# Linear attention and gated FFN on one core: a new step order from block 1 on, q's halves combined by reductions, six weight chunks reloaded

## The chip, the core and the metric

One core of a Trainium2 chip runs the whole program. Its engines work beside each other, each on its own list of instructions, in order: TensorE (PE in the profile, with PEld for its weight loads), VectorE (DVE), ScalarE (ACT), GpSimd (POOL) and SyncE (SP). Semaphores order them against each other. In this kernel SP issues loads from the inputs, writes of split weights to DRAM and writes of the output; POOL issues the loads that bring split weights back from DRAM. The metric is the device time of one launch in microseconds; 1039.9 is the median of three runs of the kernel before.

## The reference

`reference.py`, cut to what is computed (batch 8, 8 heads, 576 rows, head size 64; 4608 tokens, d_model 512, d_ff 1536; all fp32):

```python
q_s = softmax(q, axis=-1)          # over the head size
k_s = softmax(k, axis=2)           # over the 576 rows
kv = einsum('bhsd,bhde', k_s, v)   # 64 x 64 per head
x = einsum('bhsd,bhde->bhse', q_s, kv)       # laid out as 4608 x 512
xn = x / sqrt(mean(x * x) + 1e-6) * rms_g
out = (silu(xn @ w_gate) * (xn @ w_val)) @ w_out
```

Both softmaxes subtract the maximum and divide by the sum plus 1e-9.

## The kernel before

**Tiles.** The 4608 tokens are nine blocks of 512. d_ff is cut in 12 chunks of 128; a chunk holds its columns of w_gate and w_val and its rows of w_out. Operands of large matmuls are split into a high part (the value rounded to fp32r, by a copy: steps named `_hi`) and a low part (the rest, by a subtraction: steps named `_lo`), and a product is three matmuls: high x high, high x low, low x high.

**The order.** No scheduler decides at build time. A string, `ORDER`, names some 3,100 steps one after the other, and a loop calls the function of each; `tc.manual_schedule()` keeps that order on every engine. A step reads `name.numbers`, and `:A`, `:D` or `:P` at its end puts it on ACT, DVE or POOL. So the string decides both where a piece of work runs and what stands ahead of it in its engine's list. If an instruction waits, all that stands behind it on its engine waits too.

**Stages.** Blocks 0 to 2 go one by one. For block j and chunk i the number is s = 12 j + i: `f1.s.0` and `f1.s.1` (L954) are the gate and value products, 12 matmuls each; `g_mul`, `silu`, `h_mul`, `h_hi`, `h_lo` make the hidden tile h; `f2.s` (L991) adds 12 matmuls with w_out into four PSUM banks of the output. `store.j.t` (L997) then scales tile t of the four into an SBUF tile `ot`, which has **two** buffers, and SP writes it out. In block 0 the weights are also unpacked. `w_hi`, `w_lo`, `o_hi`, `o_lo` split a chunk into the tiles `w` and `o` (two buffers each), in every one of the three blocks anew. During block 1 `w_keep` and `o_keep` write the split chunks to DRAM (`wd`, `od`), and `s_add`, `s_hi`, `s_lo`, `s_keep` prepare sums of weight quarters in DRAM for what follows.

Blocks 3 to 8 go as three pairs p = 0, 1, 2, with seven products in place of eight (Strassen-Winograd). `t_add`, `b_hi`, `b_lo` build the operands from x (after `x_nm`, the product of x with the norm's row); `pp.p.i.m.k` (L1095) is product k of chunk pair i, for gate (m = 0) or value (m = 1), six matmuls. `c_s1`, `c_u2` and the other `c_` steps add products (L1116), which frees their PSUM banks. `gate`, `hm`, `hp_hi`, `hp_lo` make h, `f2p.p.t.c` (L1182) is the output product of block t of the pair with chunk c, and `put.p.t.n` copies output tile n into `ot`, with the same two buffers. `w_in` and `o_in` (L1068, L1080) bring the split weights from DRAM, issued by POOL.

**Attention beside it.** While PE is on one block, the attention of later blocks runs in between. k: `k_max` (DVE), `k_tr` (a transpose on PE), `k_top` (DVE), `k_diag` (ACT or DVE), `k_rows` (PE, L549), `k_sub`, `k_exp`, then `k_mm` (PE) makes kv. q comes in with each head's 64 numbers on two groups of 32 partitions, so its maximum and sum are found for each half (`q_max`, `q_sum`), the other half's are fetched from the neighbouring partitions by four small reductions (`q_half`, `q_half2`, L707) and the two are combined: `q_max2` (L715) by a tensor_tensor, `q_sum2` (L733) by a scalar_tensor_tensor that also adds 1e-9. `q_sub`, `q_exp`, `q_rec`, `q_mul`, `q_t`, `q_hi`, `q_lo` follow, `q_x` (PE) makes x, and `x_sq`, `x_acc`, `n_hi`, `n_lo`, `n_sum` and the `n_` steps the norm.

Of the kernel before, what the change touches and what calls it, by code (L numbers as in the profile page):

```python
# [90 lines left out]
k_eps.2.0 h_mul.12 store.0.2:A s_add.1.1:P store.0.3:D h_hi.12:A k_rec.2.0 s_hi.0.4:A q_lo.2.0:P w_hi.14.0.2:A
s_keep.0.3 f1.13.1 g_mul.13 h_lo.12:P kv_hi.2.0:A k_load.2.2 silu.13 kv_lo.2.0 s_hi.1.1:A s_lo.0.4:P o_hi.13:A f2.12
h_mul.13 w_hi.15.0.2:A w_lo.14.0:P s_keep.0.4 h_hi.13:A k_diag.2.1:A w_lo.14.1:D v_ones.2.2 v_load.2.2 s_lo.1.1:P
k_rows.2.1 o_hi.14:A f1.14.0 k_sub.2.1 o_lo.13:P k_exp.2.1 s_keep.1.1 h_lo.13:D o_keep.13 w_lo.15.0:P q_x.2.0 k_max.2.2
w_keep.14 k_mm.2.1 w_lo.15.1:P x_hi.2.0:A g_mul.14 x_sq.2.0 f1.14.1 k_load.2.3 x_lo.2.0 silu.14 s_add.1.2:P k_eps.2.1
k_rec.2.1 w_keep.15 o_lo.14:P s_hi.1.2:D kv_hi.2.1:A k_tr.2.2 f2.13 h_mul.14 s_lo.1.2:P o_keep.14 kv_lo.2.1 h_hi.14:A
k_top.2.2 s_add.1.3:P k_diag.2.2:A s_keep.1.2 h_lo.14:D v_ones.2.3 k_rows.2.2 s_hi.1.3:A f1.15.0 v_load.2.3 k_sub.2.2
s_add.1.4:P o_hi.15:A k_exp.2.2 s_lo.1.3:P w_hi.16.0.2:D f1.15.1 k_max.2.3 w_lo.16.0:P s_keep.1.3 s_hi.1.4:A g_mul.15
w_lo.16.1:P silu.15 q_sub.2.1:P k_tr.2.3 w_keep.16 k_mm.2.2 k_top.2.3 s_lo.1.4:P f2.14 k_eps.2.2 k_load.3.0 q_exp.2.1
h_mul.15 k_rec.2.2 o_lo.15:P h_hi.15:D s_keep.1.4 w_hi.17.0.2:A q_sum.2.1 h_lo.15:P o_keep.15 f1.16.0 o_hi.16:A  # L100
q_half2.2.1 k_diag.2.3:A w_lo.17.0:P kv_hi.2.2:A q_sum2.2.1 q_rec.2.1 kv_lo.2.2 w_lo.17.1:P k_rows.2.3 g_mul.16 f1.16.1
q_mul.2.1:P k_sub.2.3 w_keep.17 silu.16 s_add.2.1:D v_ones.3.0 v_load.3.0 q_t.2.1 o_lo.16:P s_hi.2.1:A f2.15 h_mul.16
q_hi.2.1:A s_lo.2.1:P w_hi.18.0.2:A k_max.3.0 q_load.3.0 h_hi.16:A q_lo.2.1:P k_exp.2.3 k_tr.3.0 f1.17.0 k_top.3.0
h_lo.16:P o_hi.17:A s_add.2.2:D k_diag.3.0:A w_lo.18.0:P s_keep.2.1 s_hi.2.2:D q_x.2.1 g_mul.17 o_keep.16 s_lo.2.2:P
k_rows.3.0 silu.17 x_hi.2.1:D f1.17.1 k_sub.3.0 w_lo.18.1:P s_keep.2.2 x_sq.2.1 s_add.2.3:D w_keep.18 k_exp.3.0
# [221 lines left out]
def linear_attention_then_gated_ffn(ctx: ExitStack, tc, q, k, v, w_gate, w_val, w_out, rms_g, out):  # L327
# [375 lines left out]

    def other_half(st):
        sw = small.tile([P, M], F32, name="sw")
        for a in range(4):
            nc.vector.tensor_reduce(out=sw[32 * (a ^ 1):32 * (a ^ 1) + 32], in_=st[32 * a:32 * a + 32].unsqueeze(2),  # L707
                                    axis=AX.X, op=ALU.max)
# [522 lines left out]
```

## Time and profile before

| what | us |
|---|---|
| median of three runs | 1039.9 |
| lowest and highest | 1037.01 and 1043.96 |
| the profiled execution | 1044.21 |
| its span, first to last instruction | 1042.5 |

The mean granted TensorE clock in the profiled execution was 0.967 of full speed. The page of the profile lists each engine's busy time and cuts the span into 40 equal slices, each a digit for tenths. The view by windows gives busy time, count of instructions and granted clock in stretches that one chooses. Timelines give start, length, engine, line, operation and tiles; the bracket behind a row tells how long the engine was idle before it and whose signal ended the wait. A group of instructions reads: busy us, mean ns of one, then idle time before them. PE's busy time is of pipelined matmuls whose ends are modelled; how fast it goes is better read from starts, as with the row of twelve matmuls that the prediction shows.

### The profile page before, as it was taken

To read this page: it belongs to the slowest core of one execution; us is meant where nothing else is said; L and a number is where in the kernel's file an instruction comes from. 1 tells how busy PE (TensorE), PEld (TensorE's weight loads), DVE (VectorE), ACT (ScalarE), POOL (GpSimd) and SP (SyncE) were. 2 spreads that over 40 slices of the span, in tenths; PEclk is the share of its full clock that TensorE was granted. 3 is DMA by queue.
4 is the path that set the end of the run, shared out by engine and by line. 5 is a ranking of instruction groups with operands and counts; after the bars stand their busy time and mean duration, and the time that the engine had idled before them with its cause. 6 is when DMAs were issued, how large, how long until landed. Compare 5 with 4: busy or idle time off the path is not lost.

```text
span 1042.5 us, 14185 instructions
## 1 busy us (share of the span) xinstructions
PE 971.2 (93%) x4681; PEld 773.5 (74%) x4681; DVE 739.7 (71%) x1460; ACT 467.3 (45%) x705; POOL 574.8 (55%) x575
## 2 busy tenths in 40 slices
PE   8999998999799898879999999979999899999997
...
PEclk8999997999899999889999999989999999999999
...
GB/s 240 246 295 159 104 87 206 330 274 236 236 163 114 132 57 108 110 174 215 205 201 192 214 231 171 166 149 196 182 190 174 232 182 223 201 186 202 117 162 141
DMA packets 164100, 192.88 MB, mean 185 GB/s; under 512 B 105620, under 2 KB 127164, under 8 KB 159420
## 3 DMA queue, kind: packets, MB, share of 16 engines
...
q8 instruction: 37, 0.61, 0.2%
...
## 4 chain that ended last, share of the span: by engine, by line
PE 56%; DVE 20%; DMA 10%; issue 5%; POOL 3%; ACT 3%; SPq 3%; DVEq 0%; POOLq 0%; ACTq 0%
PE ps_gv L1095 13%; PE ps_o L1095 10%; PE ps_gv L954 8%; PE ps_o L1182 8%; PE ps_a L1095 5%; PE ps_o L991 3%; PE ps_a L1182 3%; DMA out_dram<-ot 3%; PE ps_gv L1182 3%; DMA vt<-in_v_dram 2%; DVE hh L389 2%; DMA qt<-in_q_dram 2%; DVE tmp L1116 1%; SPq L635 1%; DVE sw L707 1%
## 5 line engine op out<-in xcount | busy, mean ns | idle before, releaser
L954 PE MATMUL ps_gv<-xh,w 128*128 128x512 f32 x576 | 198.7, 412 | 3.7 <-DVE gs L959 2.0
L1095 PE MATMUL ps_gv<-x,ring 128*128 128x512 f32 x576 | 150.1, 406 | 14.8 <-DVE tmp L1116 8.8
L1095 PEld LDWEIGHTS ps_gv<-x,ring 128*128 128x128 f32 x576 | 110.4, 195 | 40.5 <-DVE tmp L1116 10.3
L954 PEld LDWEIGHTS ps_gv<-xh,w 128*128 128x128 f32 x576 | 112.6, 196 | 31.4 <-DVE gs L966 2.3
L954 PE MATMUL ps_gv<-xl,w 128*128 128x512 f32 x288 | 116.6, 408 | 0.0
L1116 DVE TENSOR_TENSOR tmp<-tmp,ps_gv 128x512 f32<-128x512 f32 x84 | 57.3, 683 | 48.5 <-PE ps_gv L1095 47.0
L1068 POOL DMA_DIRECT2D ring<-wd x54 | 30.0, 556 | 109.4 <-PE ps_o L1095 42.9
L877 POOL TENSOR_TENSOR w<-w,w 128x512 fp32r<-128x512 f32 x61 | 82.4, 1360 | 10.2 <-ACT w L389 5.0
L1095 PE MATMUL ps_o<-x,ring 128*128 128x512 f32 x360 | 86.8, 394 | 0.0
L389 ACT CAST hh<-gs 128x512 fp32r<-128x512 f32 x38 | 23.5, 619 | 126.3 <-DVE gs L1152 104.4
L1095 PEld LDWEIGHTS ps_o<-x,ring 128*128 128x128 f32 x360 | 68.6, 191 | 14.6
L991 PE MATMUL ps_o<-o,hh 128*128 128x512 f32 x256 | 66.5, 401 | 3.1 <-ACT hh L389 2.6
L954 PEld LDWEIGHTS ps_gv<-xl,w 128*128 128x128 f32 x288 | 57.0, 198 | 11.7 <-issue 0.6
L991 PEld LDWEIGHTS ps_o<-o,hh 128*128 128x128 f32 x256 | 47.2, 189 | 14.4 <-ACT hh L389 3.0
L1080 POOL DMA_DIRECT2D o<-od x36 | 20.5, 571 | 66.4 <-PE ps_o L1182 37.6
L1116 DVE TENSOR_TENSOR tmp<-tmp,ps_o 128x512 f32<-128x512 f32 x42 | 28.7, 685 | 30.0 <-PE ps_o L1095 29.4
L1068 POOL DMA_DIRECT2D w<-wd x18 | 10.0, 555 | 60.6 <-PE ps_a L1095 35.8
L975 POOL TENSOR_TENSOR hl<-gs,hh 128x512 fp32r<-128x512 f32 x24 | 32.3, 1344 | 18.4 <-ACT hh L389 16.8
L885 POOL TENSOR_TENSOR o<-w,o 128x512 fp32r<-128x512 f32 x30 | 40.3, 1344 | 1.3 <-ACT o L389 0.8
L1182 PE MATMUL ps_o<-o,hh 128*128 128x512 f32 x144 | 38.2, 398 | 2.6 <-DVE hh L389 2.6
L520 DVE TENSOR_REDUCE cm<-kt 116x128 f32<-116x640 f32 x28 | 36.7, 1309 | 3.4 <-DMA kt<-in_k_dram 3.3
L755 POOL TENSOR_TENSOR ql<-qT,qh 128x512 fp32r<-128x512 f32 x24 | 32.2, 1345 | 11.2 <-ACT qh L389 7.2
...
## 6 DMA issues: line engine op xcount, KB each, us to landing
...
ring<-wd POOLq DMA_DIRECT2D x18, 1024.0 KB, 5.3
w<-wd POOLq DMA_DIRECT2D x18, 1024.0 KB, 5.3
...
```

Of the source, the lines that this page charges most:

```text
L389: (e.copy if e is nc.scalar else e.tensor_copy)(dst, src)
L520: nc.vector.tensor_reduce(out=cm, in_=kt_[b, g].rearrange("p h j d -> p h d j"), axis=AX.X, op=ALU.max)
L755: on(nc.gpsimd).tensor_tensor(out=ql, in0=qT_[j, g], in1=qh_[j, g][0].bitcast(F32), op=ALU.subtract)
L877: on(nc.gpsimd).tensor_tensor(out=w[:, :, 1], in0=halves(s % NF, a, 1)[:, 0], in1=w[:, :, 0].bitcast(F32), op=ALU.subtract)
L885: on(nc.vector).tensor_tensor(out=ol, in0=W(s % NF, 2), in1=oh.bitcast(F32), op=ALU.subtract)
L954: nc.tensor.matmul(pd[s], lhsT=w[:, a, c // 2, m, c % 2 * P:c % 2 * P + P], rhs=X[j, c][x], start=(n == 1), stop=(n == 3 * NKT))
L975: on(nc.gpsimd).tensor_tensor(out=hl, in0=g_[s], in1=h_[s][0].bitcast(F32), op=ALU.subtract)
L991: nc.tensor.matmul(po[t], lhsT=a[:, t * P:(t + 1) * P], rhs=w, start=(i == 0 and n == 0), stop=(i == NF - 1 and n == len(terms) - 1))
L1068: nc.gpsimd.dma_start(t, src.rearrange("p a b f -> p (a b f)"))
L1095: nc.tensor.matmul(abc[b], lhsT=src[:, h, c * P:(c + 1) * P], rhs=operand(o, c, x), start=first and n == 0, stop=n == 5, skip_group_check= ...
L1116: nc.vector.tensor_tensor(out=dst, in0=ux[u + (src,)], in1=abc[b], op=ALU.add)
L1182: nc.tensor.matmul(pa[p, t, k], lhsT=a[:, k * P:(k + 1) * P], rhs=w, start=(c == 0 and n == 0), stop=(c == NF - 1 and n == 2))
```

## The change

The constants, tile sizes, pools and all matmuls stay. Three things change.

1. `ORDER` is another list from block 1 on (the steps before `h_mul.11` are the same): other places for most steps, and other engines for some 330 of them.
2. `q_max2` and `q_sum2` become reductions: the own and the other half's numbers stand beside each other in one tile, and for the sum a third column holds 1e-9 in three tiles that are kept.
3. The steps `w_hi`, `w_lo`, `o_hi` and `o_lo` of chunks 30 to 35 (the last six of block 2) are left out of the list. In their place `w_back` and `o_back` load the split chunks that block 1 wrote to DRAM. Both functions stood in the file, unused.

```diff
-k_tr.2.0 s_add.0.1:D h_hi.11:A q_hi.2.0:A w_lo.12.1:D s_hi.0.1:A s_add.0.2:D f1.12.0 w_keep.12 s_lo.0.1:D s_hi.0.2:A
+k_tr.2.0 h_hi.11:A w_lo.12.1:D f1.12.0 w_lo.13.1:D w_keep.12 k_top.2.0 s_add.0.1:D k_diag.2.0:A w_lo.13.0:D s_hi.0.1:A
...
-hp_lo.2.1.11:D f2p.2.1.11 put.2.1.0:D put.2.1.1:A put.2.1.2:D put.2.1.3:A
+put.2.0.2:D hp_lo.2.1.11:D f2p.2.1.11 put.2.0.3:A put.2.1.0:D put.2.1.1:D put.2.1.2:D put.2.1.3:A
...
     def q_max(j, g):
-        st = small.tile([P, M], F32, name="st")
-        nc.vector.tensor_reduce(out=st, in_=qt_[j, g], axis=AX.X, op=ALU.max)
+        st = small.tile([P, M, 2], F32, name="st")
+        nc.vector.tensor_reduce(out=st[:, :, 0], in_=qt_[j, g], axis=AX.X, op=ALU.max)
         st_[j, g] = st
 
     def other_half(st):
-        sw = small.tile([P, M], F32, name="sw")
         for a in range(4):
-            nc.vector.tensor_reduce(out=sw[32 * (a ^ 1):32 * (a ^ 1) + 32], in_=st[32 * a:32 * a + 32].unsqueeze(2),
+            nc.vector.tensor_reduce(out=st[32 * (a ^ 1):32 * (a ^ 1) + 32, :, 1], in_=st[32 * a:32 * a + 32, :, :1],
                                     axis=AX.X, op=ALU.max)
-        return sw
...
     def q_max2(j, g):
-        nc.vector.tensor_tensor(out=st_[j, g], in0=st_[j, g], in1=sw_[j, g], op=ALU.max)
+        m = small.tile([P, M], F32, name="sw")
+        nc.vector.tensor_reduce(out=m, in_=st_[j, g], axis=AX.X, op=ALU.max)
+        st_[j, g] = m
...
     def q_sum(j, g):
-        sm = small.tile([P, M], F32, name="sm")
-        nc.vector.tensor_reduce(out=sm, in_=qt_[j, g], axis=AX.X, op=ALU.add)
+        n = turn["sum"] = turn.get("sum", -1) + 1
+        if n < 3:
+            SUMS.append(const.tile([P, M, 3], F32, name=f"sum_{n}"))
+            nc.gpsimd.memset(SUMS[n][:, :, 2], EPS_SUM)
+        sm = SUMS[n % 3]
+        nc.vector.tensor_reduce(out=sm[:, :, 0], in_=qt_[j, g], axis=AX.X, op=ALU.add)
         sm_[j, g] = sm
...
     def q_sum2(j, g):
-        nc.vector.scalar_tensor_tensor(out=sm_[j, g], in0=sm_[j, g], scalar=EPS_SUM, in1=sw_[j, g],
-                                       op0=ALU.add, op1=ALU.add)
+        sr = small.tile([P, M], F32, name="sm")
+        nc.vector.tensor_reduce(out=sr, in_=sm_[j, g], axis=AX.X, op=ALU.add)
+        sm_[j, g] = sr
```

The functions that the six chunks now use:

```python
    def w_back(s):
        i, odd = divmod(s % NF, 2)
        at = A21 if odd else A11
        w = w_tile(s)
        for m in range(2):
            nc.gpsimd.dma_start(w[:, m], wd[i][m][:, at:at + 2])

    def o_back(s):
        o = wsp.tile([P, 2, DM], F32R, name="o")
        nc.gpsimd.dma_start(o, od[s % NF])
        wo_[s] = [o[:, 0], o[:, 1]]
```

What the table moves is shown at three places. The first is the end of block 2, where DVE copies out its four tiles (`ot<-ps_o,yt`) while pair 0 has begun. Before:

```order
L707 TENSOR_REDUCE sw<-sm 32x16 x4
L396 TENSOR_SCALAR ot<-ps_o,yt 128x512
L585 TENSOR_SCALAR rs<-ps_a 128x1
L733 SCALAR_TENSOR_TENSOR sm<-sm,sw 128x16
L396 TENSOR_SCALAR ot<-ps_o,yt 128x512
L1116 TENSOR_TENSOR tmp<-tmp,ps_gv 128x512
```

and now (line numbers shift by two to five in the changed file; L394 is the old L396, L1121 the old L1116):

```order
L798 TENSOR_TENSOR acc<-acc,sq 128x512
L1121 TENSOR_TENSOR tmp<-tmp,ps_gv 128x512
L394 TENSOR_SCALAR ot<-ps_o,yt 128x512 x2
L518 TENSOR_REDUCE cm<-kt 116x128
L1121 TENSOR_TENSOR tmp<-tmp,ps_gv 128x512 x2
```

Before, DVE had the first and the last of the four copies, with the other two on ACT between them; now it has the first two, and the last two stand later on ACT. The second place is POOL around chunk 33 of block 2 (`wd` and `od` are the split weights in DRAM, `hl` h's low part, `qt` the exponentials of q, `vt` v's tile). Before:

```order
L885 TENSOR_TENSOR o<-w_95,o 128x512
L1014 TENSOR_TENSOR xh<-xh,r 128x512
L877 TENSOR_TENSOR w<-w_96,w 128x2x256
L975 TENSOR_TENSOR hl<-gs,hh 128x512
L877 TENSOR_TENSOR w<-w_96,w 128x2x256
L740 TENSOR_TENSOR qt<-qt,sm 128x512
L885 TENSOR_TENSOR o<-w_96,o 128x512
```

and now:

```order
L911 DMA w<-wd_0_126 128x1024
L911 DMA w<-wd_1_127 128x1024
L514 MEMSET vt 116x10
L745 TENSOR_TENSOR qt<-qt,sm 128x512
L980 TENSOR_TENSOR hl<-gs,hh 128x512
L915 DMA o<-od_138 128x1024
```

The subtractions that made the low parts of `w` and `o` (L877, L885) have gone from POOL's list, and the issues of three loads stand there.

The third place is k's chain on PE in block 2: the transpose `k_tr` (L535, now L533) gives DVE the tile for a maximum, ACT or DVE makes a diagonal (`cm`) of it, and `k_rows` (L549, now L547) multiplies that by ones. Before:

```order
L766 MATMUL ps_a<-ql,kv_hi_106 128x384
L535 MATMUL ps_a<-ident,cm 128x116
L954 MATMUL ps_gv<-xh,w 128x512
L954 MATMUL ps_gv<-xl,w 128x512
...
L954 MATMUL ps_gv<-xh,w 128x512 x4
L549 MATMUL ps_a<-cm,ones 116x128
```

and one of them now:

```order
L996 MATMUL ps_o<-o,hl 128x512 x4
L533 MATMUL ps_a<-ident,cm 128x116
L547 MATMUL ps_a<-cm,ones 116x128
L771 MATMUL ps_a<-qh,kv_hi_102 128x256
L771 MATMUL ps_a<-qh,kv_lo_103 128x256
```

Before, twelve matmuls of 512 columns stood between the two; here nothing does.

More of the change, by code (lines that the diff above doesn't have):

```diff
@@ L91 @@
[L91 to L105, printed above, removed]
@@ L321 @@
-hp_hi.2.1.9:D o_in.2.1.11 hp_lo.2.1.9:D f2p.2.1.9 hp_hi.2.1.10:D hp_lo.2.1.10:D f2p.2.1.10 hp_hi.2.1.11:D
-hp_lo.2.1.11:D f2p.2.1.11 put.2.1.0:D put.2.1.1:A put.2.1.2:D put.2.1.3:A
+k_tr.2.0 h_hi.11:A w_lo.12.1:D f1.12.0 w_lo.13.1:D w_keep.12 k_top.2.0 s_add.0.1:D k_diag.2.0:A w_lo.13.0:D s_hi.0.1:A
+n_t.1 s_add.0.2:P k_rows.2.0 w_keep.13 f1.12.1 k_sub.2.0 s_lo.0.1:P s_hi.0.2:A n_y0.1 k_exp.2.0 n_y1.1 h_lo.11:P
+s_keep.0.1 f2.11 kv_lo.1.2:P q_hi.2.0:A n_rows.1 s_add.0.3:P g_mul.12 s_lo.0.2:P k_tr.2.1 k_mm.2.0 store.0.0:A
@@ new lines @@
+x_sq.3.0 q_exp.4.0 q_lo.3.1:P n_y1.2 o_hi.24:A k_tr.3.2 s_lo.4.4:P k_top.3.2 o_lo.24:P s_keep.4.4 store.1.0:A
+k_diag.3.2:A k_max.3.3 store.1.1:A k_rows.3.2 q_x.3.1 o_hi.25:A k_sub.3.2 s_lo.5.1:P q_sum2.3.2 k_exp.3.2 q_rec.3.2
+n_rows.2 x_cp.3.1:A q_mul.3.2:P k_mm.3.2 s_keep.5.1 g_mul.24 x_sq.3.1 q_sum.3.3 o_lo.25:P silu.24 q_t.3.2 k_tr.3.3
+k_load.4.0 f1.25.0 k_eps.3.2 s_add.5.3:P q_half2.3.3 k_rec.3.2 k_top.3.3 q_load.4.1 v_ones.4.0 k_diag.3.3:D s_hi.5.3:A
+h_mul.24 kv_hi.3.2:A s_lo.5.2:D q_hi.3.2:A s_add.5.4:D q_lo.3.2:P k_rows.3.3 x_acc.3.1:P g_mul.25 f1.25.1 v_load.4.0
```

448 lines of the change are left out of this document (228 added, 220 removed).

## The prediction

> **What bounds the kernel now.** I read the page first: busy shares and the granted clock.
>
> ```profile
> PE 971.2 (93%) x4681; PEld 773.5 (74%) x4681; DVE 739.7 (71%) x1460; ACT 467.3 (45%) x705; POOL 574.8 (55%) x575
> ...
> PE   8999998999799898879999999979999899999997
> ...
> PEclk8999997999899999889999999989999999999999
> ```
>
> TensorE (PE) is the bound, and the notches in its row return as notches in the clock row. So a stall is paid twice: as idle time, then at a lower granted clock. Next came the table by stage, cut at places of the program: 148.4 is the first matmul step of block 1 (f1.12.0), 234.7 is f1.20.0, 451.7 is pp.0.1.0.1, 488.6 is pp.0.2.0.1, 677.5 is pp.1.1.0.1, 814.3 is f2p.1.0.11, 849.2 is pp.2.0.0.1.
>
> ```profile
> core 0: us, PE busy (x) PEld busy (x) DVE busy (x) ACT busy (x) POOL busy (x), PEclk, DMA share, GB/s
> 0.00:148.40 148.40, 140.84 (x709) 102.92 (x709) 119.58 (x238) 116.19 (x181) 121.35 (x122) 0.98 0.68 188
> 148.40:199.20 50.80, 44.11 (x222) 33.98 (x221) 33.77 (x65) 30.27 (x44) 36.15 (x31) 0.87 0.71 247
> 199.20:234.70 35.50, 35.39 (x177) 28.93 (x176) 31.32 (x52) 28.29 (x38) 34.10 (x29) 1.00 0.85 289
> 234.70:451.70 217.00, 192.38 (x1002) 152.80 (x1001) 198.36 (x432) 121.27 (x172) 156.83 (x135) 0.94 0.49 144
> 451.70:488.60 36.90, 30.71 (x148) 24.82 (x146) 26.32 (x59) 19.43 (x29) 18.83 (x22) 0.91 0.78 210
> 488.60:523.10 34.50, 30.45 (x163) 23.99 (x163) 28.48 (x69) 16.94 (x23) 15.71 (x19) 0.95 0.76 202
> ...
> 677.50:690.50 13.00, 5.95 (x18) 4.50 (x17) 7.33 (x8) 2.74 (x5) 5.00 (x5) 0.74 0.49 146
> 690.50:814.30 123.80, 122.71 (x542) 101.20 (x540) 65.31 (x102) 25.68 (x43) 37.88 (x48) 1.00 0.61 189
> 814.30:849.20 34.90, 32.27 (x133) 25.89 (x134) 20.61 (x34) 3.44 (x6) 9.54 (x14) 0.95 0.64 197
> 849.20:999.70 150.50, 150.16 (x661) 123.62 (x660) 69.58 (x105) 22.61 (x37) 28.41 (x41) 1.00 0.57 177
> ```
>
> Two kinds of loss stand out. Between 234.7 and 451.7 VectorE (DVE) is 91% busy (198.36 of 217.00) while PE idles 24.6 us: there DVE sets the pace. Elsewhere the losses are short and deep, as 677.5 to 690.5, where every engine idles at once; the steady stretches before and after it (690.5 to 814.3, 849.2 to 999.7) lose next to nothing. The view of the output tile `ot` and the timelines around the deep notches name their cause.
>
> ```profile
> its engine sat idle before it (us, times) until:
>   DMA out_dram<-ot: 71.1, 16
> ```
>
> ```profile
> 172.00 0.75 DVE L396 TENSOR_SCALAR ot<-ps_o,yt 128x512 f32<-128x512 f32 x1 [7.47 <-DMA out_dram<-ot]
> ...
> 170.27 1.99 PE L991 MATMUL ps_o<-o,hh 128*128 128x512 f32 x6 [2.55 <-ACT hh L389]
> 172.81 1.22 PE L991 MATMUL ps_o<-o,hh 128*128 128x512 f32 x2 [0.55 <-DVE ot L396]
> ...
> 457.99 0.75 DVE L396 TENSOR_SCALAR ot<-ps_o,yt 128x512 f32<-128x512 f32 x1 [5.37 <-DMA out_dram<-ot]
> 458.66 0.68 DVE L1116 TENSOR_TENSOR tmp<-tmp,ps_gv 128x512 f32<-128x512 f32 x1
> ...
> 459.39 2.93 PE L1095 MATMUL ps_gv<-x,ring 128*128 128x512 f32 x6 [6.19 <-DVE tmp L1116]
> ...
> 684.60 0.69 DVE L389 COPY ot<-ps_gv 128x512 f32<-128x512 f32 x1 [5.67 <-DMA out_dram<-ot]
> ...
> 686.04 0.77 PE L766 MATMUL ps_o<-qh,kv_hi 128*128 128x512 f32 x1 [7.05 <-DVE tmp L1116]
> ...
> 825.66 1.59 PE L1182 MATMUL ps_o<-o,hh 128*128 128x512 f32 x5 [2.59 <-DVE hh L389]
> ```
>
> Four tiles of output are stored after each block, and `ot` has two buffers. The third store stands right behind the second on an in-order engine, so that engine waits until an output DMA has landed, and all its later work waits too. At 457.99 DVE has stood 5.37 us, then runs the 0.68 us addition (L1116) that frees the PSUM bank, and PE has lost 6.19 us. The bracket on PE names DVE; the DMA is behind it.
>
> **The change, part by part.** *The stores move apart.* At the end of block 2 (rows with the change) DVE now writes the two tiles that find free buffers and goes on to a reduction and L1121 (the old L1116); the third and fourth stand on ScalarE (ACT), further on. What the distance is worth follows from these rows: how long an output DMA takes, and what twelve matmuls take.
>
> ```profile
> 454.94 2.95 DMA out_dram<-ot
> ...
> 678.96 5.52 DMA out_dram<-ot
> ...
> 850.70 2.72 PE ps_gv L1095 x12
> ```
>
> Counted along the new order at 2.72 us for twelve matmuls, the matmul work between second and third store grows from nothing or 1.4 us to 5.7 us after block 0, 4.9 after block 2, and 8.2 after each of pair 0's second and pair 1's first output. Against landings of 2.95 to 5.52 us all four waits should go, the second narrowly. What they cost is PE's idle time plus the clock that the stage lost, length times (1 - PEclk). Block 2's: 6.19 + 0.09 x 36.9 = 9.5. Pair 0's: 7.05 + 0.26 x 13.0 = 10.4. Pair 1's: 2.59 + 0.05 x 34.9 = 4.3. Block 0's: 2.55 + 0.55 = 3.1 of the 6.7 us that PE idles in that stage, and the same share of 0.13 x 50.8 = 6.6, so 3.1 + 3.1 = 6.2. Together 30.4. I take **-28**, because of the narrow one; bounds -32 (shorter waits at the other stores go too) and -18 (the later copies hold PSUM banks that the next matmuls want, and the two largest waits come back by a third).
>
> *Less on DVE in the stretch that it bounds.* The rows of the kinds that leave and come:
>
> ```profile
> L389 DVE CAST hh<-gs 128x512 fp32r<-128x512 f32 x30 | 26.8, 895 | 0.6
> ...
> L707 DVE TENSOR_REDUCE sw<-sm 32x16 f32<-32x16 f32 x112 | 18.0, 161 | 2.1
> ...
> L733 DVE SCALAR_TENSOR_TENSOR sm<-sm,sw 128x16 f32<-128x16 f32 x28 | 14.7, 523 | 0.4
> L715 DVE TENSOR_TENSOR st<-st,sw 128x16 f32<-128x16 f32 x28 | 14.3, 510 | 0.2
> ...
> L389 DVE CAST w<-w 128x1024 fp32r<-128x1024 f32 x5 | 6.0, 1194 | 0.0
> ...
> L1014 DVE TENSOR_TENSOR xh<-xh,r 128x512 f32<-128x512 f32 x1 | 1.8, 1771 | 0.0
> ...
> L1014 DVE TENSOR_TENSOR xl<-xl,r 128x512 f32<-128x512 f32 x1 | 0.7, 679 | 0.0
> ```
>
> Combining two halves of 128x16 took 0.51 us, although a reduction of 32x16 takes 0.16. The new form reduces 16x2 or 16x3 numbers, so I estimate 0.18 and 0.19 from L707. Between f1.20.0 and pp.0.1.0.1 the order puts 14 and 15 of these on DVE where 12 and 13 stood: 5.4 instead of 12.9, -7.5 us. Seven of eight casts of h go to ACT (-7 x 0.895 = -6.3), and the four weight casts there are the reloaded chunks' (-4 x 1.194 = -4.8). Four more products of x with r come in (+4 x 1.225, the mean of the last two rows, = +4.9). The remaining kinds, each counted at its mean, give about -7. Net -21. At DVE's 91% nearly all of that is time, but the stretch ahead (199.2 to 234.7, where PE idles 0.1 us) gets 8 us more DVE work, which puts DVE's 31.3 at 39 against 35.5 us: +4. So **-16**; bounds -21 and 0 (DVE's whole load from 148.4 to 523.1 falls by only 10). From 488.6 to 523.1 DVE loses 7 us of 28.5 and PE has 4.1 us idle and 1.7 of clock to win: **-4**, bounds -5 and 0.
>
> Here a rule bears on the row. The Trainium skill (SBUF — State Buffer, Who interferes with whom) says that a DVE instruction with two SBUF inputs waits for a GpSimd instruction that reads SBUF, and that a tensor_reduce never does. The rows agree (0.51 against 0.16). By that rule the change also works against itself: on DVE from 148.4 to 523.1 it has 8 more weight subtractions and 6 more sums with two SBUF inputs, which would take up part of the 7.5, and the sum would be some 4 us worse.
>
> *Chunks 30 to 35 of the weights come from DRAM.* As the rows with the change show, three subtractions per chunk on POOL become three DMA issues.
>
> ```profile
> L877 POOL TENSOR_TENSOR w<-w,w 128x512 fp32r<-128x512 f32 x61 | 82.4, 1360 | 10.2 <-ACT w L389 5.0 <-DVE rs L585 3.9 <-issue 0.7
> ...
> L1068 POOL DMA_DIRECT2D w<-wd x18: 530/534/602, 404.6 to 966.3; - x18
> ...
> w<-wd POOLq DMA_DIRECT2D x18, 1024.0 KB, 5.3
> ```
>
> POOL gives back about 18 x (1.36 - 0.53) = 15 us; it doesn't bound, so I count nothing. What hides the loads: a chunk's buffer is free after f1 of the chunk two earlier, and until its use PE has two halves of f1 and two of f2 steps, 4 x 2.72 = 10.9 us. Two issues and a landing take 2 x 0.53 + 5.3 = 6.4. So **0**, with 4.5 us of slack; behind a waiting issue stand q's products and h's low halves on POOL. Bounds 0 and +4.
>
> *What gets tighter.* k's chain (transpose on PE, maximum on DVE, diagonal on ACT, row sums on PE) loses cover: from block 2 on, no k_rows stood less than 1.4 us of matmuls behind its k_tr, now three stand at 0.1 and two under 1. Before:
>
> ```profile
> PE ps_a L549 <- ACT cm L394: 7.8, 6, 2.3
> ```
>
> That is 1.3 us a time. Five such waits and some shorter ones: **+9**, bounds 0 (they fall where PE would wait for DVE anyway) and +14. *The tail.* Three of pair 2's first four outputs now leave with the last matmul step, so seven copies share two buffers around PE's end, not four. One more landing stands in the chain:
>
> ```profile
> 1036.32 2.21 DMA out_dram<-ot
> ```
>
> **+2.5**, bounds 0 and +4. Sum: -28 - 16 - 4 + 0 + 9 + 2.5 = **-36.5**. The profiled execution took 1044.2 (span 1042.5 and 1.7 around it), 4.3 over the median of 1039.9; taken from the median, that gives **1003**.
>
> **Rivals.** *Only the stores help.* DVE's load falls by 10 of some 330 us from 148.4 to 523.1; if it still sets the pace, its two terms halve (-10) and k's waits cost 12: -28 - 10 + 12 + 2.5 = -23.5, **1016**. For it: DVE is 91% busy. Against it: the load is now spread more evenly. *The waits come back.* Stores apart keep their banks and buffers longer; half of the 28 returns and DVE's relief is eaten by k's waits: -14 - 10 + 14 + 4 = -6, **1034**. *The reload is late (slower).* It decides when POOL reaches an issue more than 4.5 us after the buffer is free; beyond that each us is PE's, plus about half again for the clock. To end over 1050 it has to undo 36.5 and add 11: 8 us a chunk over six chunks, so POOL 10 us behind at each (5.3 late x 1.5 = 8). The row of 530 to 602 ns an issue speaks against it. The Trainium skill (SBUF — State Buffer, the section on the wrong bandwidth-pool intuition) has a POOL-issued DMA stretched from about 620 to 3100 ns beside a DVE copy; by that estimate two issues cost 5 us more, a chunk is 0.5 us late and the time is 1006. No issue in the row is stretched so. *More goes well.* k's waits are hidden and all gains reach their bounds: -32 - 21 - 5 + 0 + 2.5 = -55.5, **984**.
>
> **How the numbers follow.** A measurement of this kernel tells about 1% from no change. Forecast (993 to 1010) 0.52, only the stores (1010 to 1028) 0.24, waits come back (1028 to 1045) 0.13, slower 0.04, more goes well (under 993) 0.07. Faster by over 1% means under 1029.5: 0.52 + 0.24 + 0.07 = 0.83. Within 1%: 0.13. Slower: 0.04. The range leaves out the two outer cases and most of "waits come back": 986 to 1029.
>
> **What would show it.** Right: the wait of `ot` for out_dram falls from 71 us to under 30; PE's waits of 6.2 and 7.1 us for L1116 (now L1121) are gone, with their low clock; the combining reductions take under 0.2 us; DVE's share between f1.20.0 and pp.0.1.0.1 stays near 90% in a stretch of some 200 us instead of 217. Wrong: PE waits for `w` out of DRAM, for L549's row sums over 15 us in all, or for the late output copies' banks.

## The result and the profile after

| | median us | runs | ratio to before, 95% interval |
|---|---|---|---|
| before | 1039.3 | 1037.0 to 1044.0 | |
| changed | 991.3 | 988.6 to 994.4 | 0.953 [0.949, 0.958] |

The change made the kernel 48 us faster. The profiled execution took 989.84 us with a span of 988.1. The two profiled spans differ by 54.4, more than the medians, because the execution of before that was profiled was a long one (1044.21) and this one a short one. The page of the changed kernel:

```profile
PE 950.7 (96%) x4681; PEld 765.5 (77%) x4681; DVE 692.1 (70%) x1435; ACT 449.3 (45%) x710; POOL 540.3 (55%) x566
...
PE   7999998899999999899999999999999999999997
...
PEclk8999999999999999899999999999999999999999
```

Nearly all notches are gone from PE's row, and the clock row has lost them too. The table by stage, cut at the same steps of the program (f1.12.0, f1.16.0, f1.20.0, pp.0.1.0.1, pp.0.2.0.1, pp.0.3.0.1, then pp.1.1.0.1, f2p.1.0.11, pp.2.0.0.1):

```profile
151.20:196.20 45.00, 38.81 (x200) 30.95 (x199) 36.83 (x78) 26.62 (x38) 30.78 (x28) 0.96 0.78 271
196.20:232.00 35.80, 35.80 (x194) 29.42 (x193) 33.59 (x63) 25.46 (x39) 23.66 (x21) 1.00 0.80 271
232.00:436.40 204.40, 191.15 (x1040) 153.66 (x1039) 178.29 (x441) 130.96 (x207) 144.14 (x141) 0.97 0.76 211
436.40:462.70 26.30, 26.30 (x136) 21.40 (x136) 22.44 (x53) 13.84 (x21) 9.76 (x14) 1.00 0.78 210
462.70:491.80 29.10, 29.10 (x182) 23.46 (x181) 19.99 (x50) 12.65 (x19) 10.23 (x13) 1.00 0.93 262
641.50:654.50 13.00, 13.00 (x59) 10.78 (x58) 8.41 (x12) 2.21 (x4) 6.11 (x6) 1.00 0.39 125
...
766.60:796.50 29.90, 29.90 (x133) 24.77 (x132) 17.61 (x31) 5.34 (x9) 12.93 (x17) 1.00 0.81 251
```

Each row answers to one of before: 50.8 us have become 45.0, 217.0 have become 204.4, 36.9 have become 26.3, 34.5 have become 29.1. In the 13 us after pp.1.1.0.1 PE now is busy all the time, where it was for 5.95. In the rows from 436.4 on, which hold the later notches, PE's busy time is the whole of the stretch. The view of `ot` has this in place of 71.1 us in 16 waits:

```profile
its engine sat idle before it (us, times) until:
  DMA out_dram<-ot: 19.7, 8
```

Two stretches of different orders don't hold quite the same matmuls (136 records against 148 in the one after pp.0.1.0.1). So that kernels can be compared, I worked out the time that PE lost: a stretch's length minus its matmuls, each priced at the 30th percentile of the distance from its start to the next start, by step and shape, in the trace of before. For the stretches that matter, in us (named by the step that begins them; the second ends at pp.0.0.0, the third to fifth at the next of their kind, the others at f1.16.0, pp.1.0.0, pp.1.2.0 and pp.2.0.0; the last column is the whole program, of use for differences: another choice of where to begin moves every row of it by the same 6.4 us):

| kernel | f1.12.0 | f1.20.0 | pp.0.0.0 | pp.0.1.0 | pp.0.2.0 | f2p.0.0.11 | pp.1.1.0 | f2p.1.0.11 | all |
|---|---|---|---|---|---|---|---|---|---|
| before | 16.6 | 39.3 | 12.0 | 10.5 | 8.7 | 5.1 | 9.3 | 4.9 | 143.5 |
| changed | 11.0 | 30.4 | 6.3 | 1.5 | 3.1 | 0.1 | 0.0 | 0.0 | 88.1 |
| stores_apart | 16.2 | 32.9 | 11.6 | 8.8 | 9.3 | 6.1 | 1.8 | 1.5 | 125.8 |
| four_buffers | 8.6 | 34.1 | 11.9 | 4.7 | 9.2 | 3.4 | 1.8 | 0.9 | 111.7 |
| combine_only | 16.3 | 31.5 | 13.4 | 10.4 | 6.4 | 5.4 | 10.0 | 4.1 | 134.3 |
| engines_only | 12.4 | 46.0 | 14.7 | 11.0 | 7.2 | 13.7 | 0.8 | 3.6 | 159.4 |
| after_old_engines | 8.7 | 44.1 | 10.2 | 1.5 | 4.0 | 7.0 | 0.0 | 0.0 | 117.5 |
| places_only | 12.8 | 44.4 | 8.4 | 2.9 | 3.5 | 4.3 | 0.5 | 0.0 | 110.2 |
| after_adjacent | 12.2 | 30.7 | 8.6 | 2.9 | 3.2 | 4.3 | 0.5 | 0.0 | 97.7 |
| after_split | 12.5 | 37.5 | 7.2 | 1.5 | 3.1 | 0.1 | 0.0 | 0.0 | 97.3 |
| after_old_combine | 12.6 | 30.8 | 6.2 | 1.5 | 3.1 | 0.1 | 0.0 | 0.0 | 85.9 |
| after_four_buffers | 5.6 | 30.8 | 6.3 | 1.5 | 6.7 | 0.1 | 0.0 | 0.0 | 82.7 |

The gain sits where the forecast had put it, at the ends of the blocks and in the stretch from f1.20.0 to pp.0.1.0. A part of that stretch's difference is chance: four_buffers has the order of before there and stores_apart that order but for two stores, and they lose 33 to 34 us where before's profiled execution lost 39.

### The profile page after: what moved, and what is told of

It reads as the page before. It is cut to its first block, busy times and chain, and to the rows that moved or that the text cites. A ratio compares the mean times of both kernels' runs of the same rounds, so it can differ in the third digit from the quotient of the medians.

```text
span 988.1 us, 14153 instructions
## 1 busy us (share of the span) xinstructions
PE 950.7 (96%) x4681; PEld 765.5 (77%) x4681; DVE 692.1 (70%) x1435; ACT 449.3 (45%) x710; POOL 540.3 (55%) x566
## 4 chain that ended last, share of the span: by engine, by line
PE 76%; DVE 8%; DMA 5%; issue 3%; POOL 2%; ACT 2%; SPq 2%; DVEq 0%; ACTq 0%; POOLq 0%
PE ps_gv L1100 17%; PE ps_o L1100 12%; PE ps_gv L959 11%; PE ps_o L1187 10%; PE ps_o L996 6%; PE ps_a L1100 6%; PE ps_a L1187 5%; PE ps_gv L1187 5%; SPq L633 1%; PE ps_a L565 1%; DMA out_dram<-ot 1%; PE ps_a L771 1%; DMA vt<-in_v_dram 1%; POOL w L449 1%; DMA kt<-in_k_dram 1%
## 5 line engine op out<-in xcount | busy, mean ns | idle before, releaser
L959 PE MATMUL ps_gv<-xh,w 128*128 128x512 f32 x576 | 196.1, 407 | 6.6 <-DVE gs L971 3.3
L1100 PE MATMUL ps_gv<-x,ring 128*128 128x512 f32 x576 | 145.2, 396 | 3.5 <-DVE tmp L1121 1.5
L959 PEld LDWEIGHTS ps_gv<-xh,w 128*128 128x128 f32 x576 | 111.2, 193 | 33.6 <-issue 5.2
L1100 PEld LDWEIGHTS ps_gv<-x,ring 128*128 128x128 f32 x576 | 107.7, 189 | 27.3 <-DVE tmp L1121 1.9
L1121 DVE TENSOR_TENSOR tmp<-tmp,ps_gv 128x512 f32<-128x512 f32 x84 | 57.3, 683 | 59.3 <-PE ps_gv L1100 52.3
L996 PE MATMUL ps_o<-o,hh 128*128 128x512 f32 x256 | 65.4, 397 | 0.0
L959 PEld LDWEIGHTS ps_gv<-xl,w 128*128 128x128 f32 x288 | 56.3, 196 | 11.6 <-issue 0.6
L882 POOL TENSOR_TENSOR w<-w,w 128x512 fp32r<-128x512 f32 x41 | 55.1, 1352 | 8.4 <-ACT w L387 4.2
L1121 DVE TENSOR_TENSOR tmp<-tmp,ps_o 128x512 f32<-128x512 f32 x42 | 28.7, 684 | 40.1 <-PE ps_o L1100 36.9
L387 ACT CAST hh<-gs 128x512 fp32r<-128x512 f32 x47 | 28.9, 616 | 61.3 <-DVE gs L971 24.8
L996 PEld LDWEIGHTS ps_o<-o,hh 128*128 128x128 f32 x256 | 46.9, 188 | 10.2 <-issue 0.4
L996 PE MATMUL ps_o<-o,hl 128*128 128x512 f32 x128 | 35.3, 398 | 2.1 <-DVE hl L980 2.1
L1187 PE MATMUL ps_o<-o,hh 128*128 128x512 f32 x144 | 37.2, 390 | 0.0
L1100 PE MATMUL ps_a<-x,w 128*128 128x512 f32 x144 | 37.0, 392 | 0.0
L1100 PE MATMUL ps_a<-x,ring 128*128 128x512 f32 x144 | 37.0, 392 | 0.0
```

Of the source, the lines that this page charges most:

```text
L387: (e.copy if e is nc.scalar else e.tensor_copy)(dst, src)
L882: on(nc.gpsimd).tensor_tensor(out=w[:, :, 1], in0=halves(s % NF, a, 1)[:, 0], in1=w[:, :, 0].bitcast(F32), op=ALU.subtract)
L959: nc.tensor.matmul(pd[s], lhsT=w[:, a, c // 2, m, c % 2 * P:c % 2 * P + P], rhs=X[j, c][x], start=(n == 1), stop=(n == 3 * NKT))
L996: nc.tensor.matmul(po[t], lhsT=a[:, t * P:(t + 1) * P], rhs=w, start=(i == 0 and n == 0), stop=(i == NF - 1 and n == len(terms) - 1))
L1100: nc.tensor.matmul(abc[b], lhsT=src[:, h, c * P:(c + 1) * P], rhs=operand(o, c, x), start=first and n == 0, stop=n == 5, skip_group_check= ...
L1121: nc.vector.tensor_tensor(out=dst, in0=ux[u + (src,)], in1=abc[b], op=ALU.add)
```

## The experiments

Twelve kernels, in three sets of four; the kernel before was timed again beside each set (medians 1042.9, 1041.3 and 1042.2).

**stores_apart.** Of the whole change, only the places of 14 stores (block 2's shown):

```diff
-store.2.0:D store.2.1:A pp.0.0.1.4 q_lo.5.2:P k_eps.5.2 q_sum2.5.3 store.2.2:A store.2.3:D pp.0.0.1.3
+store.2.0:D store.2.1:A pp.0.0.1.4 q_lo.5.2:P k_eps.5.2 q_sum2.5.3 pp.0.0.1.3
...
+pp.0.1.0.6 store.2.2:A
...
+pp.0.1.0.2 store.2.3:D
```

> Before, with only the third and fourth copy into ot of seven output groups moved behind the matmul steps that they follow in the changed kernel (their engines as before; pair 2's stay). Theory 'the waits for an output buffer are most of the gain, whatever else stands in the order': the four deep notches (block 0, block 2, pair 0's second, pair 1's first output) go, 25 to 31 us less, ratio 0.970 to 0.976, and DVE's and ACT's wait of ot for out_dram falls from 71 us to under 30. Rival 'it takes the rest of the new order': without it the later copies hold the PSUM banks that the next matmuls want, half of that comes back, 12 to 15 us less, ratio 0.986 to 0.988, with PE waiting for ot.

Measured: 1027.3 us, ratio 0.987 [0.984, 0.990]; the wait for out_dram fell to 45.8 us. The rival was right in size, though not by its mechanism alone. Pair 0's and pair 1's notches went (9.3 to 1.8, 4.9 to 1.5), block 0's stayed (16.6 to 16.2) and so, nearly, did block 2's (10.5 to 8.8). Why block 2's stayed is in the timelines of SP, ACT and PE:

```profile
444.08 3.78 SPq L638 DMA_DIRECT2D qt<-in_q_dram  x8
447.97 7.44 SPq L1001 DMA_DIRECT2D out_dram<-ot  x3
...
454.36 0.69 ACT L397 ACTIVATE ot<-ps_o,yt 128x512 f32<-128x512 f32 x1 [5.63 <-DMA out_dram<-ot]
...
456.16 0.46 PE L538 MATMUL ps_a<-ident,cm 116*128 116x116 f32 x1 [3.65 <-ACT sq L786]
```

DVE and ACT had finished the first two copies at 445.6, but SP, in order too, was still issuing a load of q, eight times, and came to the output at 447.97. By then POOL had issued one load of split weights, at 446.02, and it issued another at 448.04, so the late output had both beside it. The third copy started on ACT 6.4 us after the output's first issue, and behind it on ACT stood a square of x for which PE waited 3.65 us.

In block 0 the four copies start at 163.7, 166.8, 169.7 and 172.6, each 2.2 to 2.3 us after the issue of the output before it: every store waited for the one right before, as if one buffer were free, and distance between the second and the third could not help. The other buffer was taken. The kernel keeps `kv_full`, the normalized kv of the first two batches, in buffers of the same name `ot`, and `kv_lo.1.2` and `kv_lo.1.3` on POOL read the second batch's at 225.9 and 232.9, long after the stores. The changed order puts `kv_lo.1.2` ahead of the stores and `kv_lo.1.3` close behind them, and the fourth copy waits for just that read (timelines of POOL and DVE in the changed kernel):

```profile
171.62 0.46 POOL L601 TENSOR_TENSOR kv_lo<-ot,kv_hi 128x128 fp32r<-128x128 f32 x1
```

```profile
163.68 0.75 DVE L394 TENSOR_SCALAR ot<-ps_o,yt 128x512 f32<-128x512 f32 x1 [3.41 <-DMA out_dram<-ot]
...
172.12 0.75 DVE L394 TENSOR_SCALAR ot<-ps_o,yt 128x512 f32<-128x512 f32 x1 [2.17 <-POOL kv_lo L601]
```

So in block 0 the two buffers are one until that read is done. The changed kernel still pays for it: its second copy waits 3.41 us for the first output, and PE then waits 2.79 us for a product (L971) that stands behind that copy on DVE.

**four_buffers.** Before, with no step moved:

```diff
-        ot = fp.tile([P, DM], F32, name="ot", bufs=2)
+        ot = fp.tile([P, DM], F32, name="ot", bufs=4)
...
```

The same number changes in the three other places that take a buffer of this name.

> Before, with four buffers for ot in place of two and nothing moved. Theory 'the third store waits for the landing of the first because there are only two buffers': the 71 us of waits for out_dram go to under 10, and the time falls by as much as in stores_apart or some us more, 25 to 33 us, ratio 0.968 to 0.976. Rival 'the copies are slow to leave for another reason (the queue that issues the output, the bank)': the waits stay or PE still stops 5 to 7 us at pp.0.1 and q_x.8.3, ratio 0.99 to 1.00.

Measured: 1008.3 us, ratio 0.969 [0.966, 0.972]. In the view of `ot` no wait for out_dram is left among the three largest:

```profile
its engine sat idle before it (us, times) until:
  PE ps_gv L1185: 32.0, 2
  PE ps_o L1185: 11.0, 4
  PE ps_a L1185: 3.5, 2
```

The theory was right: with buffers enough, the waits go and 33 us with them. That is what the waits cost in the old order, twice what moving the stores took back. In block 0 three copies go at once and the fourth waits 1.67 us for an output, as it must with `kv_full` in one of four buffers.

**combine_only** and **apart_and_combine.** `q_max2` and `q_sum2` as reductions, on the old order and with the stores apart; the edit is that of the diff above.

> Before, with q_max2 and q_sum2 as reductions and nothing moved. DVE gets 29.0 - 28 x (0.177 + 0.195) = 18.6 us shorter. Theory 'DVE sets the pace from 234.7 to 451.7': 25 of the 56 stand there, 25 x 0.33 = 8 us less, ratio 0.992. Rival 'the lock only moves': the next two-input instruction on DVE waits for POOL in their place, and DVE's total falls by less than 6 us, ratio 0.998 to 1.000.

> Before, with both of these edits (stores moved apart, reductions), order otherwise as before. If the two gains stand for themselves they add: 28 + 8 = 36 us less, ratio 0.965, which leaves 12 us of the change's 48 to the rest of the new order and the reload. If DVE's relief only counts where the stores don't stop it, or the rest of the order carries it, under 28 us less, ratio over 0.973.

Measured: 1038.3 us, ratio 0.997 [0.995, 0.999], and 1023.4 us, ratio 0.982 [0.979, 0.984]. Alone the reductions are worth about 4 us, between theory and rival, and with the stores apart they add about as much (0.987 to 0.982, with intervals that just touch). The stores and the reductions together left 28 of the 48 us unexplained.

**after_old_combine.** The changed order, with the old forms of both:

```diff
-        nc.vector.tensor_reduce(out=m, in_=st_[j, g], axis=AX.X, op=ALU.max)
+        nc.vector.tensor_tensor(out=st_[j, g], in0=st_[j, g], in1=sw_[j, g], op=ALU.max)
...
-        nc.vector.tensor_reduce(out=sr, in_=sm_[j, g], axis=AX.X, op=ALU.add)
+        nc.vector.scalar_tensor_tensor(out=sm_[j, g], in0=sm_[j, g], scalar=EPS_SUM, in1=sw_[j, g],
+                                       op0=ALU.add, op1=ALU.add)
```

> The changed kernel with q_max2 as a tensor_tensor and q_sum2 as a scalar_tensor_tensor again, order and all else as changed. Alone on the old order the reductions gave 3.5 us, with the stores apart 3.9 us. Theory 'the same few us in any order, since only some of the 56 stand where DVE sets the pace': 3 to 5 us over the changed kernel, 995, ratio to before 0.957. Rival 'the new order is laid out for shorter instructions on DVE': 8 us or more over it, 1000, ratio over 0.960. The forecast's 7.5 us for this part speaks for the rival.

Measured: 989.8 us, ratio 0.949 [0.946, 0.953], no slower than the changed kernel. Its groups, and then those of the changed kernel:

```profile
L716 DVE TENSOR_TENSOR st<-st,sw 128x16 f32<-128x16 f32 x28 | 15.4, 548 | 0.4
...
L734 DVE SCALAR_TENSOR_TENSOR sm<-sm,sw 128x16 f32<-128x16 f32 x28 | 9.5, 341 | 0.4
```

```profile
L738 DVE TENSOR_REDUCE sm<-sum 128x16 f32<-128x48 f32 x28 | 5.4, 195 | 0.6
L712 DVE TENSOR_REDUCE sw<-st 128x16 f32<-128x32 f32 x28 | 4.9, 177 | 0.4
```

The old forms cost DVE 24.9 us against 10.3, and the time shows nothing of it (f1.20.0 to pp.0.0.0 loses 30.8 us against 30.4). Both expectations were wrong: in the new order the 14.6 us must lie beside matmuls that don't wait for them.

**after_split.** The changed kernel, with chunks 30 to 35 split on the chip again:

```diff
-w_back.30
+w_hi.30.0.2:A w_lo.30.0:P w_lo.30.1:P
...
-o_back.30
+o_hi.30:A o_lo.30:P
```

> The changed kernel with chunks 30 to 35 split on the chip again (high part by a copy, low part by a subtraction, on the engines of before, where the changed order has the reloads); one load of a chunk's output rows, o_in.0.0.1, stands later, since it uses the space that the unsplit chunks then still hold. This puts back 4 casts of 1.19 us and one subtraction on DVE, 17 subtractions of 1.35 us on POOL, 5 casts of 0.6 us and 2 of 1.05 us on ACT. Theory 'the reload buys nothing but POOL time that wasn't short' (the forecast counted 0): within 3 us of the changed kernel, ratio to before 0.953 to 0.956. Rival 'it relieves a stretch in which every engine is near full': 5 to 10 us over it, ratio 0.958 to 0.963.

Measured: 999.4 us, ratio 0.960 [0.956, 0.963], 6 (by the ratios, whose intervals overlap a little) to 8 us (by the medians) over the changed kernel, as the rival had it. But a part of that is my placing. Its timelines of PE and POOL:

```profile
333.47 2.07 PE L963 MATMUL ps_gv<-xh,w 128*128 128x512 f32 x4 [2.98 <-POOL w L886]
...
328.67 2.52 POOL L886 TENSOR_TENSOR w<-w,w 128x512 fp32r<-128x512 f32 x2 [2.77 <-ACT w L391]
331.15 1.05 POOL L749 TENSOR_TENSOR qt<-qt,sm 128x512 f32<-128x512 f32 x1
332.15 1.26 POOL L886 TENSOR_TENSOR w<-w,w 128x512 fp32r<-128x512 f32 x1
```

The two subtractions of chunk 30 stood where the reload had stood, ahead of the last one of chunk 29, and PE waited 2.98 us for that one. The windows from f1.28.0, f1.30.0 and f1.32.0 to the next of these steps and to f1.34.0, first here and then in the changed kernel:

```profile
318.40:342.60 24.20, 21.22 (x111) 17.44 (x110) 16.96 (x49) 15.74 (x25) 19.01 (x17) 0.93 0.46 105
342.60:367.00 24.40, 21.61 (x126) 17.15 (x125) 20.53 (x55) 13.92 (x23) 17.48 (x14) 0.93 0.27 60
367.00:391.80 24.80, 21.85 (x124) 17.24 (x123) 19.74 (x59) 16.94 (x23) 21.64 (x22) 0.93 0.30 68
```

```profile
322.30:342.10 19.80, 19.80 (x110) 16.46 (x109) 16.49 (x44) 13.57 (x21) 16.80 (x18) 0.98 0.74 179
342.10:362.80 20.70, 19.86 (x126) 15.91 (x125) 19.61 (x57) 13.52 (x22) 13.14 (x18) 1.00 0.80 216
362.80:384.00 21.20, 20.12 (x125) 16.02 (x124) 16.21 (x53) 15.02 (x21) 15.39 (x18) 1.00 0.89 210
```

The first of them, with that wait, is 4.4 us longer, and much of that comes from where I put the splits. The other two are 3.7 and 3.6 us longer, with POOL busier by 4.3 and 6.3 us. From f1.24.0 to pp.0.0.0 as a whole it is 7.1 us, since the stretches before and after these three came out shorter. So the reload is worth at most 8 us; how much of it is left with a better placing, no run shows.

**after_adjacent.** The changed kernel, third and fourth store behind the second again and ten of the copies back on the engines of before:

```diff
-store.2.0:D hm.0.0.22:P store.2.1:D pp.0.0.1.3
+store.2.0:D hm.0.0.22:P store.2.1:A store.2.2:A store.2.3:D pp.0.0.1.3
```

> The changed kernel with the third and fourth store of seven groups right behind the second again, on the engines of before. Theory 'the spacing itself is what the waits hang on': 25 to 30 us over the changed kernel, 1018, ratio to before 0.977 to 0.982. Rival from stores_apart (the spacing is worth 15 us there, and at block 2 the copies still waited 5.6 us because SP issued the output 2.9 us late, behind eight issues of a load of q): with SP free at that moment the adjacent stores wait less, 2.5 to 3 us each, and the spacing is worth 10 to 15 us here too, ratio 0.963 to 0.968.

Measured: 999.1 us, ratio 0.957 [0.954, 0.961], 4 us over the changed kernel by the ratios, whose intervals overlap, and 8 by the medians: less than either theory or rival. The surprise is that the waits did come back:

```profile
its engine sat idle before it (us, times) until:
  DMA out_dram<-ot: 58.9, 17
```

Many of them cost nothing: in the table this kernel loses 2.9, 0.5 and 0.0 us where the kernel before lost 10.5, 9.3 and 4.9. Pair 0's second output shows how. The chain, the timelines of DVE and of PE in after_adjacent:

```profile
649.22 2.05 DMA out_dram<-ot
```

```profile
651.39 0.69 DVE L390 COPY ot<-ps_gv 128x512 f32<-128x512 f32 x1 [2.20 <-DMA out_dram<-ot]
...
647.45 6.99 PE L1103 MATMUL ps_o<-x,ring 128*128 128x512 f32 x30
654.66 1.65 PE L1103 MATMUL ps_o<-x,ring 128*128 128x512 f32 x6 [0.22 <-DVE tmp L390]
```

The landing took 2.05 us where it took 5.52 before, and PE had thirty matmuls that needed nothing of DVE. POOL's timelines, before and then after_adjacent, give what differs:

```profile
678.04 0.59 POOL L1068 DMA_DIRECT2D ring<-wd  x1 [0.26 <-issue]
```

```profile
643.45 0.53 POOL L1076 DMA_DIRECT2D w<-wd  x1 [3.10 <-PE ps_o L824]
```

Before, a load of weights was issued at 678.04 and the output at 678.96. The DMA queues of before from 679.0 to 682.3 then moved these packets alone:

```profile
q0 software_dynamic: 112, 0.69, 92.8%
```

They are all of POOL's queue, and none is of SP's output (queue q1), which had been issued at their start. In after_adjacent the last load was issued 5.8 us ahead of the output, and the 2.2 us from its issue on have packets of q1 alone.

**after_four_buffers.** The edit of four_buffers on the changed kernel.

> The changed kernel with four buffers for ot. If spacing has taken nearly all of the waits: block 0's 3.4 us and the 8 us at the end are what is left, of which PE feels 3 to 6 us, 986 to 988, ratio to before 0.948 to 0.951. If nothing of them lies on PE's path: no difference, ratio 0.953.

Measured: 983.2 us, ratio 0.942 [0.938, 0.947]: better than expected, and faster than both kernels. Block 0's stretch lost 5.6 us where the changed kernel lost 11.0. Beside it the waits can be priced in both orders: none to 58.9 us of them is 16 us here (983.2 to 999.1, which takes back both the buffers and the spacing), and 1.7 to 71.1 is 33 to 35 in the old order (1008.3 to 1042.9).

**apart_outputs_first.** stores_apart, and what stood ahead of the outputs on SP moved:

```diff
-q_load.6.1 store.2.0:D store.2.1:A
+store.2.0:D store.2.1:A q_load.6.1
...
-put.0.1.0:D put.0.1.1:A
+put.0.1.1:A put.0.1.0:D
```

> stores_apart with two more moves, both of what stands ahead of an output on SP: the eight issues of a load of q (3.78 us on SP) go behind block 2's second store, and of pair 0's second output the tile that ACT has ready is issued ahead of the one that DVE copies 5.7 us later. Theory 'the third copy waits for a landing, and the landing is late because SP issues the first two late': at block 2 the waits of 5.6 and 2.5 us fall by about 2.9 each and the stretch from pp.0.1 to pp.0.2 goes from 35.2 to 31 or 32 us; 3 to 6 us less than stores_apart's 1027, ratio 0.981 to 0.984. Rival 'the transfers themselves are slow there': the waits stay within 1 us, ratio 0.987 as in stores_apart.

Measured: 1028.7 us, ratio 0.987 [0.983, 0.990], no different from stores_apart. The theory was right on the wait and wrong on the time: the waits of 5.6 and 2.5 us at block 2 went to zero, out_dram's sum fell from 45.8 to 35.1, and the stretch hardly got shorter (34.1 against 35.2 us). Its clock rose from 0.90 to 1.00:

```profile
446.30:480.40 34.10, 29.04 (x146) 22.54 (x145) 26.18 (x59) 19.31 (x29) 18.61 (x22) 1.00 0.86 227
```

```profile
445.10:480.30 35.20, 31.17 (x146) 24.41 (x146) 26.33 (x59) 19.39 (x29) 18.83 (x22) 0.90 0.82 220
```

PE now waited 1.53 us for the fourth copy's bank, 1.81 for k's diagonal and 1.35 for k's exponentials, in place of one wait of 3.65. Where one wait went, others came up. The two rows also bear on how the prediction priced a stall: PE idles 5.1 us in the first, in shorter pieces, at a clock of 1.00, and 4.0 us in the second at 0.90. So idle time isn't always paid a second time in the clock.

**engines_only, after_old_engines, places_only.** Before with 317 steps on the engines of the changed kernel; the changed kernel with those 317 on the engines of before; and the changed order and engines with all three named parts undone (old combining, split chunks, adjacent stores). One step as an example of the 317:

```diff
-c_s1.0.1.0:D
+c_s1.0.1.0:A
```

> Before, with 317 steps on the engines that the changed kernel gives them; places, stores, reductions and reload as before. Theory 'the rest of the gain is that DVE gets less to do where it sets the pace': the stretch from f1.20 to pp.0.1 gets 8 to 12 us shorter, ratio 0.988 to 0.992. Rival 'engines and places only fit each other': on the old places the moved steps come late for those behind them, ratio 0.998 to 1.01.

> The changed kernel with those 317 steps on the engines of before. Theory 'engines': 8 to 15 us over the changed kernel, 999 to 1006, ratio to before 0.960 to 0.967. Rival 'engines and places only fit each other': 20 us or more over it, ratio over 0.972. If the places alone carry it, ratio 0.953 to 0.957.

> The changed order and engines, but the three named parts undone together: q combined by the old forms, chunks 30 to 35 split on the chip, third and fourth stores right behind the second. If the parts add up as they stood one by one (reductions 0, reload 8, spacing 8), 1007, ratio to before 0.968: then two thirds of the gain are in neither of them but in where the other steps stand. If they stand in for each other (each undone part is covered while the others are there), over 1015, ratio over 0.976.

Measured: 1056.9 us, ratio 1.014 [1.011, 1.018]; 1019.0 us, ratio 0.978 [0.974, 0.981]; 1012.2 us, ratio 0.971 [0.967, 0.975]. The new engines on the old places make the kernel 15 us slower, more than the rival had expected, though DVE has less to do, as the page of engines_only says:

```profile
PE 969.1 (92%) x4681; PEld 772.7 (73%) x4681; DVE 714.4 (68%) x1442; ACT 483.2 (46%) x736; POOL 557.2 (53%) x562
```

That is 25 us less on DVE than before, and 16 more on ACT. The old engines on the new places cost 25 (by the ratios) to 28 us, as that rival said. places_only, finally, is 30 us faster than before with no reduction, reload or spacing in it, near what adding up predicts. Its stretches after pp.0.1.0.1 and pp.1.1.0.1, and from f2p.1.0.11 on, with the stores adjacent as before:

```profile
451.70:479.40 27.70, 26.82 (x136) 21.28 (x135) 24.51 (x55) 12.79 (x19) 9.71 (x14) 1.00 0.75 199
662.50:687.60 25.10, 24.87 (x110) 20.19 (x109) 14.73 (x19) 5.01 (x9) 13.79 (x14) 1.00 0.62 215
788.20:818.10 29.90, 29.90 (x133) 24.77 (x132) 18.04 (x31) 5.34 (x9) 13.46 (x17) 1.00 0.83 255
```

PE loses 2.9, 0.5 and 0.0 us there, although the view of `ot` has 60.8 us of waits for out_dram in this kernel.

## Why the prediction was right, and where not

The time, 991.3, lies in the range of 986 to 1029, and just below the 993 to 1010 of the likeliest case, in the band of the rival "more goes well". Of that rival's conditions one came true (k's waits cost nothing); DVE's gain did not reach its bound. Term by term:

- **Stores, -28.** By place and sum right: the stretches after f1.12.0, pp.0.1.0, pp.1.1.0 and from f2p.1.0.11 lost 5.6, 9.0, 9.3 and 4.9 us less, 28.8 together, against 6.2, 9.5, 10.4 and 4.3 counted. The cause was wrong in part. "Against landings of 2.95 to 5.52 us all four waits should go" took the landing as given and the matmuls between the stores as what decides. Spacing alone gave 15 us on the old order, and the new order without spacing keeps most of the gain: after_adjacent loses only 1.2, 1.4, 0.5 and 0.0 us more than the changed kernel at these four places. So that the sum fits is in part luck. In block 0 the step "`ot` has two buffers" failed too, as `kv_full` held one of them. What a wait cost also hung on when SP came to the issue, on the load in flight beside it, and on what stood behind the waiting copy. The rival "the waits come back" was right for stores_apart, but held banks were not all of it.
- **DVE's stretch, -16.** It fell by 12.6 us (217.0 to 204.4), and DVE's busy time there by 20.1 (198.36 to 178.29) against the 21 counted. The step that failed is "at DVE's 91% nearly all of that is time", and with it the 7.5 us of the reductions: they measured 0.177 and 0.195 us as estimated, and were worth about 4 us on the old order and nothing that shows in the new one. engines_only says the same from the other side: less on DVE, more time. A part of the 12.6 is also that before's profiled execution was slow in that stretch. The 4 us counted against it in the stretch ahead didn't come: 35.5 us became 35.8, with DVE busy for 33.6 and not 39. And "DVE's whole load from 148.4 to 523.1 falls by only 10" was too little: summed over the rows of these stages it fell by 27 (318.2 to 291.1).
- **From 488.6, -4.** 34.5 us became 29.1: -5.4, with DVE busy for 8.5 us less where 7 were counted. That DVE's load is the cause isn't shown: places_only, with the old reductions, loses 3.5 us there against 3.1.
- **The reload, 0.** No load was late: PE waits for none, the issues took 530 to 602 ns and the landings at most 7.4 us. The source view of `w_back` has these rows (the longest are of `o_back`).

```profile
L911 POOL DMA_DIRECT2D w<-wd x12: 535/556/593, 330.1 to 383.5; - x12
...
DMA to landing us min/median/max: 4.2/4.9/6.8
```

  But "it doesn't bound, so I count nothing" of POOL's 15 us was too strict: after_split puts it at up to 8 us, a part of it my placing. The Trainium skill (SBUF — State Buffer, the section on the wrong bandwidth-pool intuition) has an issue beside a DVE copy stretched to some 3100 ns; the longest issue of a weight load in this trace takes 766 ns.
- **k's chain, +9.** This failed. The waits at the three pairs that now stand next to each other are there (0.97, 1.16 and 1.90 us), but the working counted the waits that come and not those that go: 2.27, 1.32, 1.58 and 1.28 us at four places of before are gone. PE's waits for the diagonal, 7.8 us in six before, are now:

```profile
PE ps_a L547 <- ACT cm L392: 5.4, 5, 1.9
...
PE ps_a L547 <- DVE cm L394: 1.1, 1, 1.1
```

  The sum is no higher (6.5 us), so the term is 0, and that is 9 of the 12 us by which 1003 was too much.
- **The tail, +2.5.** Three output landings of about 2 us stand at the end of the chain, as forecast. From the last matmul's end to the span's end 5.4 us became 6.4, and the matmuls ahead of it took 1.8 us less, so that the end as a whole costs nothing. In after_four_buffers no landing stands between the last matmul and the last copy.
- **Not in the sum:** pair 0's first output, whose third copy now stands behind 2.7 us more of matmuls, lost 5.1 us before and 0.1 now; in the new order with adjacent stores it is 4.3, so here the spacing did it, but only with the new engines (after_old_engines, with the same spacing, loses 7.0).

So the number came out near because the stalls had been priced at their places from PE's idle time and clock, whatever removed them, and because not all errors went one way: DVE's term was some 4 us too good, while k's chain, the tail and the missing term for pair 0's first output were 9, 3 and 5 too bad. What removed the stalls is settled only in part: the three named parts together are worth 18 (by the ratios) to 21 us (1012.2 to 991.3) and the new places with their engines 27 to 30. Which of the moved steps, SP's loads among them, carry those isn't settled: no run moved the loads alone within the new order.
